# Linear attention and two MoE layers on one core: program order for the regular part of layer 1, with side work, stores and a weight reload moved

## The chip, the core and the metric

The kernel runs on one core of a Trainium2 chip. The metric is the device time of one execution in microseconds, lower is better. The core has five engines with a queue of instructions each: TensorE (PE; its weight loads are listed apart, as PEld), VectorE (DVE), ScalarE (ACT), GpSimd (POOL) and SyncE (SP). SyncE and GpSimd issue the DMA transfers here. Engines wait for each other by semaphores; an engine that waits holds up everything behind it in its own queue.

## The reference

Three stages follow each other on 4608 tokens (8 batches of 576) of 512 features (8 heads of 64).

```python
kv  = einsum('bhsd,bhse->bhde', k, v)          # 64 x 64 for each batch and head
out = einsum('bhsd,bhde->bhse', q, kv)
x   = out / sqrt(mean(out * out, -1) + 1e-6) * g_norm
h = x @ w_in;   x = (h * sigmoid(1.702 * h)) @ w_out       # layer 1, 512 to 2048 to 512
h = x @ w2_in;  y = (h - tanh(h)) @ w2_out                 # layer 2, the same sizes
```

## The kernel before, in words

**Tiles.** A tile is one batch, 576 tokens. For each of the two layers (`l`) and eight tiles (`n`) the kernel runs two matrix products on TensorE: `m1` (line 520, called M1 here) multiplies by w_in and `m2` (line 635, M2) by w_out. Each takes seven products of sums of quarters in place of eight quarter products, and each of those is made in three fp16 passes (high by high, high by low, low by high). M1 and M2 each have 336 matmuls of 128x128 by 128x288; these are called regular matmuls here. They add up in the PSUM banks `X`, `Y` and `Z`, two of each. Tile (0,0) is computed by plain products (`m1_plain`, `m2_plain`). Tiles are written (layer, number); the regular part of layer 1 is (0,2) to (0,7).

**M2.** It has 28 steps of 12 matmuls (line 680 on), four for each of the products 2, 1, 5, 6, 7, 3, 4 in this order (`ORDER2`); products 2 and 3 add up in Y, 5 in Z, the others in X. The weights come from DRAM as 14 blocks of 512 KB into four buffers `st` (`stream`, line 629, issued on SyncE). Each block serves two steps, 24 matmuls; when its steps are written, the next block that uses its buffer is issued (`FREED2`):

```python
for _ in range(min(FREED2.get(i, 0), 14 - len(pre))):
    pre.append(stream(l, len(pre)))
```

The operand `jt` comes from the activations `gt` by ScalarE (line 605) and VectorE (line 611). In layer 1 results go to `x2d` in DRAM by `store` (line 641, SyncE), and `x2load` (line 340, SyncE) brings them back for layer 2.

**Attention as side work.** While M2 of tile n of layer 1 runs, `front` (line 364) does the first half of the attention for tile n + 2, in four units of two heads: k-by-v products (line 385, 10 passes on TensorE), copies of the result to `kv` (lines 388 and 389, ScalarE), numerators q by kv (line 397), their squares rounded and exact (lines 409 and 410, ScalarE), the difference of the two (line 413, VectorE), sums of the squares over features as matmuls with `sel` (line 421), mean squares (line 424), and after the last unit the roots. While M1 of tile n + 1 runs, `back` (line 473) does the second half: `newton` (lines 441 to 450, the last of its steps gives `hl`, line 449), spreads of the inverse roots over the features (line 456, TensorE, bank `AT`), products with the numerators (line 460), and `xprep` (line 306), which writes the fp16 operand `xo` of the next M1. K-by-v products, numerators, sums and spreads share the two banks `AT`.

**Layer 2's weights.** `conv1` (line 191) converts them during layer 1, 32 items with loads and stores on GpSimd's queue and their arithmetic mostly on VectorE. When M2 of (0,7) has been written, the eight tiles `wi` of w_in are reloaded with layer 2's (line 949, SyncE).

**Order.** Side work is made of generators. `add_side(g, a, b)` registers one, and `tick` lets it advance `a` times in each step of M1 and `b` times in each step of M2; a `yield` in a generator thus sets a distance in steps. `issue_after` keeps a piece of side work behind marked main instructions. `drain` runs a generator to its end. What is written in this order is then placed by a scheduler, engine by engine, except where `tc.manual_schedule(engines=...)` is entered: there the named engines keep the order of the program. Before the change that holds for TensorE and SyncE in layer 2 alone:

```python
if l == 1:
    ...
    man.enter_context(tc.manual_schedule(engines=frozenset([mybir.EngineType.PE, mybir.EngineType.SP])))
```

Of the kernel before, what the change touches and what calls it, by code (L numbers as in the profile page):

```python
# [8 lines left out]
F32 = mybir.dt.float32  # L9
# [73 lines left out]
def body(ctx, tc, att, gn, con, w_in, w_out, w2_in, w2_out, outT):  # L83
# [279 lines left out]

    def front(b, places=None, banks=None):

        if not places and b not in ahead:
            yield from fetch(b)  # L370
        for u, (kt, i) in enumerate(UNITS):
# [4 lines left out]
            K = A[u % 2]  # L376
            if places:
                unit = places[u]
                q, kv = unit[:, 0:T], unit[:, T:UNIT]
            else:  # L380
                qb, kb = ahead[b]
                q, kv = qb.ap, kb.ap
            kv = kv.rearrange("p (w c d) -> p w c d", w=2, c=5)
# [5 lines left out]
            nc.scalar.copy(out=d[64:128, 64:128], in_=K[64:128, 64:128])  # L389
            if not places:  # L390
                kb.free()
                if u < 3:
                    kb = yield from part(b, u + 1, T, UNIT)
            yield
            yield
            for j in range(2):
                nc.tensor.matmul(out=A[j][:, 0:H], lhsT=d, rhs=q[:, j * H:(j + 1) * H], start=True, stop=True)
            if places:
                sq = unit[:, T:2 * T]
            else:  # L400
                qb.free()
                if u < 3:
                    qb = yield from part(b, u + 1, 0, T)
                    ahead[b] = qb, kb
                ex = yield from scr.need(T)
                sq = ex.ap
            for j in range(2):
# [5 lines left out]
            nc.vector.tensor_tensor(out=slr, in0=sq, in1=shr.bitcast(F32), op=ALU.subtract)  # L413
            if not places:
                ex.free()
            yield
# [8 lines left out]
            yield  # L425
            if b == 0 and u % 2:
                yield u // 2
        if b:
            y = yield from scr.need(H)
            t = yield from scr.need(H)  # L430
            yt[:] = y, t
            roots(slice(0, P))
            nc.scalar.activation(out=dummy, in_=t.ap[:, 0:1], func=AF.Gelu_apprx_sigmoid)
        yield
# [38 lines left out]
    def back(b, dst):  # L473

        hi, hl = shr[:, 0:H], slr[:, 0:H]
        yield from newton(slice(0, P), hi, hl)
        for x in yt:
            x.free()
        for u, (kt, i) in enumerate(UNITS):
            yield from scaled_unit(b, u, hl, slice(0, P), AT)  # L480
            if i == 1:
                ex = yield from scr.need(3 * H)
                yield from xprep(xbs[b, kt], ex, dst[:, kt])
                if kt == 0 and b < NS - 1:
                    yield from fetch(b + 1)


# [147 lines left out]
    def m2(l, n, tails, pre):  # L635
# [5 lines left out]
        def store(qd, ob, ds):  # L641

            m, j = qd // 2, qd % 2
            src = ob.ap[:, :T].rearrange("p (d f) -> p d f", d=2)[:, ds]
            dst = (x2d if l == 0 else outT.rearrange("(k p) f -> k p f", p=P))
            dst = dst[2 * m:2 * m + 2, :, n * T + j * H:n * T + (j + 1) * H].rearrange("d p f -> p d f")[:, ds]
            main((nc.sync if l == 0 or n == NS - 1 else nc.gpsimd).dma_start(out=dst, in_=src))

# [10 lines left out]
        def quad(qd, d, name):  # L659
# [4 lines left out]
            if d == 1:  # L664
                cc.pop(name).free()

        def fin(r, d):
# [16 lines left out]
            elif r == 4:  # L684
                scaled(x, d, 4)
                quad(2, d, 4)

        for i in range(28):
            r, pp = STEPS2[i]
            s = pre[ORDER2.index(r) * 2 + pp // 2]  # L690
# [16 lines left out]
            for _ in range(min(FREED2.get(i, 0), 14 - len(pre))):  # L707
                pre.append(stream(l, len(pre)))
            if i == 0:
                tail1()  # L710
            elif i == 1:
                tail2()
            elif i == 2:
                flush()
                flush()
                jcap[0] = 28
            jadvance(i + 1 + LA)
            tick(1)


# [130 lines left out]
    def both0():  # L851

        yt[:] = scr(H), scr(H)
        chains = [front(0, room, banks)]
        while chains:
# [20 lines left out]
    for l in range(2):  # L876
        for n in range(NS):
            bk = fr = None
            if l == 0:
# [4 lines left out]
                elif n < NS - 1:  # L884
                    bk = add_side(back(n + 1, xo[(n + 1) % 2]), 0.6, 1.0)
                else:
# [3 lines left out]
            if (l, n) == (0, 2):  # L890
                add_side(later, 0.85, 0.0)

# [15 lines left out]
            if l == 1:  # L908
                fixed[0] = True
                marks.clear()  # L910
                marks.update({k: m for k, m in latest.items() if k == mybir.EngineType.DVE})
                man.enter_context(tc.manual_schedule(engines=frozenset([mybir.EngineType.PE, mybir.EngineType.SP])))
            if (l, n) == (0, 0):
# [28 lines left out]
            if l == 0 and 1 <= n < NS - 2:  # L942
                drain([bk])
                fr = add_side(front(n + 2), 0.0, 1.1)
            m2(l, n, tails, pre)
            if l == 0 and n == NS - 1:
                drain([later])
                for p in range(NP):
                    nc.sync.dma_start(out=wi[p], in_=wid[p])
            drain([bk, fr])  # L950
# [42 lines left out]
```

## Time and profile before

| | us |
|---|---|
| time, median of 3 runs | 1516.06 |
| lowest and highest of the runs | 1514.57, 1516.18 |
| the profiled execution | 1515.95 |
| its span | 1514.2 |
| TensorE busy | 1459.4 (96%) |
| VectorE busy | 1184.3 (78%) |
| ScalarE busy | 945.7 (62%) |
| GpSimd busy | 134.7 (9%) |
| mean DMA rate | 155 GB/s |

How to read it: the span is the part of the profiled execution from its first to its last instruction, and all places in the trace are microseconds from its start. Busy shares are averages over stages; a stage is read from a window that is cut at its first and last matmul. The records of TensorE overlap, since a matmul of 0.29 us starts every 0.12 us; the distance of starts is what one costs. The column PEclk is the clock that TensorE was granted, as a share of 2.4 GHz: 1.00 is that level and 0.50 is 1.2 GHz. A wait is put down to the instruction that came last.

### The profile page before, as it was taken

Reading aid. Unit: us, or ns where it says so; the run is one execution under the profiler, and the core shown is the slowest. Engines: PE = TensorE matmul, PEld = TensorE weight load, DVE = VectorE, ACT = ScalarE, POOL = GpSimd, SP = SyncE. Lnnn points to the kernel's source line nnn. Section 1 sums busy time; section 2 is a strip of 40 time slices with the busy share of each in tenths; the row PEclk is TensorE's granted clock in tenths of the full one; section 3 lists DMA queues with packets and bytes.
Section 4 is the critical chain, followed back from the end, with each engine's and each line's share of the span. In section 5 each row is a group of like instructions: output and inputs, shape, how many; then the busy total and the mean of one; then the engine's idle time right before and its main releaser. Section 6 shows DMA issues by size and latency. Waiting matters only on the chain.

```text
span 1514.2 us, 29446 instructions
## 1 busy us (share of the span) xinstructions
PE 1459.4 (96%) x11508; PEld 1159.8 (77%) x11508; DVE 1184.3 (78%) x2357; ACT 945.7 (62%) x2075; POOL 134.7 (9%) x209
## 2 busy tenths in 40 slices
PE   6979799999999999999999999999999999999999
PEld 5667577777787877877677777777777777777777
DVE  4999979497796987959858686877777787868585
ACT  5766586676777767767556465646565565656463
POOL 0000010022223221211100000000000000000000
PEclk8899899999999999999999999999999999999999
DMA  8684415447567475672576415070614333241504
GB/s 310 208 249 128 147 62 196 140 132 250 165 209 234 128 253 178 199 237 70 185 250 231 148 59 192 15 231 22 195 56 156 111 118 125 86 142 44 184 15 157
DMA packets 96525, 235.36 MB, mean 155 GB/s; under 512 B 10112, under 2 KB 49152, under 8 KB 96384
## 3 DMA queue, kind: packets, MB, share of 16 engines
q1 hardware_dynamic: 78848, 165.95, 34.1%
q0 software_dynamic: 17536, 67.51, 13.4%
q8 instruction: 90, 1.47, 0.4%
q14 instruction: 51, 0.42, 0.1%
HBM read 191.48 MB, written 41.94 MB: 154 GB/s over the span
## 4 chain that ended last, share of the span: by engine, by line
PE 78%; DMA 8%; DVE 8%; ACT 3%; issue 3%; POOL 0%; SPq 0%; ACTq 0%; DVEq 0%; POOLq 0%
PE X L530 7%; PE X L702 7%; PE X L704 7%; PE X L703 7%; PE X L532 7%; PE X L531 7%; PE Y L702 4%; PE Y L704 4%; PE Y L703 4%; PE Z L530 3%; PE Z L532 3%; PE Z L531 3%; DMA st<-wod 3%; PE Z L702 2%; PE Z L704 2%
## 5 line engine op out<-in xcount | busy, mean ns | idle before, releaser
L611 DVE SCALAR_TENSOR_TENSOR jt<-gt,jt 128x576 f16<-128x576 f32 x420 | 312.6, 753 | 106.9 <-ACT jt L605 103.1
L605 ACT ACTIVATE jt<-gt 128x576 f16<-128x576 f32 x420 | 284.6, 684 | 156.0 <-PE X L704 56.6
L530 PE MATMUL X<-xo,wi 128*128 128x288 f16 x960 | 274.6, 286 | 7.4 <-ACT mscratch L563 4.7
L531 PE MATMUL X<-xo,wi 128*128 128x288 f16 x960 | 274.7, 286 | 2.1 <-DVE xo L323 2.1
L532 PE MATMUL X<-xo,wi 128*128 128x288 f16 x960 | 274.6, 286 | 0.0
L703 PE MATMUL X<-jt,st 128*128 128x288 f16 x960 | 274.2, 286 | 0.0
L704 PE MATMUL X<-jt,st 128*128 128x288 f16 x960 | 274.0, 286 | 0.0
L702 PE MATMUL X<-jt,st 128*128 128x288 f16 x960 | 273.4, 286 | 0.0
L702 PEld LDWEIGHTS <-st 128*128 128x128 f16 x1680 | 165.0, 98 | 60.8 <-DMA st<-wod 17.2
L563 ACT COPY mscratch<-X 128x288 f32<-128x288 f32 x360 | 141.2, 396 | 106.1 <-PE X L532 92.6
L531 PEld LDWEIGHTS <-wi 128*128 128x128 f16 x1680 | 164.7, 98 | 50.4 <-issue 8.2
L530 PEld LDWEIGHTS <-wi 128*128 128x128 f16 x1680 | 164.5, 98 | 47.1 <-issue 4.4
L703 PEld LDWEIGHTS <-st 128*128 128x128 f16 x1680 | 165.1, 98 | 43.4
L704 PEld LDWEIGHTS <-st 128*128 128x128 f16 x1680 | 165.2, 98 | 43.4 <-issue 0.3
L532 PEld LDWEIGHTS <-wi 128*128 128x128 f16 x1680 | 164.5, 98 | 44.3 <-issue 2.5
L591 DVE TENSOR_TENSOR gt<-gt 128x576 f32<-128x576 f32 x240 | 176.7, 749 | 1.4 <-ACT gt L537 1.1
L702 PE MATMUL Y<-jt,st 128*128 128x288 f16 x480 | 136.2, 289 | 10.3 <-DMA st<-wod 10.3
L568 DVE TENSOR_TENSOR mscratch<-Z,mscratch 128x288 f32<-128x288 f32 x240 | 108.1, 452 | 38.5 <-ACT mscratch L563 22.2
L703 PE MATMUL Y<-jt,st 128*128 128x288 f16 x480 | 137.9, 288 | 0.0
L704 PE MATMUL Y<-jt,st 128*128 128x288 f16 x480 | 137.5, 288 | 0.0
L530 PE MATMUL Z<-xo,wi 128*128 128x288 f16 x480 | 137.5, 286 | 0.0
L531 PE MATMUL Z<-xo,wi 128*128 128x288 f16 x480 | 137.4, 286 | 0.0
(238 smaller groups left out, 2572.0 us busy)
## 6 DMA issues: line engine op xcount, KB each, us to landing
st<-wod SPq DMA_DIRECT2D x210, 512.0 KB, 4.7
scratch<-att POOLq DMA_DIRECT2D x28, 640.0 KB, 4.8
scratch<-x2d SPq DMA_DIRECT2D x32, 288.0 KB, 5.9
cbk<-w_out POOLq DMA_DIRECT2D x32, 256.0 KB, 4.3
cbk<-w_in POOLq DMA_DIRECT2D x32, 256.0 KB, 4.1
scratch<-att POOLq DMA_DIRECT2D x28, 288.0 KB, 4.5
x2d<-mscratch SPq DMA_DIRECT2D x28, 288.0 KB, 5.4
outT<-mscratch POOLq DMA_DIRECT2D x28, 288.0 KB, 5.0
```

The source lines that it names most:

```text
L530: nc.tensor.matmul(out=out, lhsT=wh, rhs=xh, start=fresh and kt == 0, stop=False, skip_group_check=k)
L531: nc.tensor.matmul(out=out, lhsT=wh, rhs=xl, start=False, stop=False, skip_group_check=k)
L532: nc.tensor.matmul(out=out, lhsT=wl, rhs=xh, start=False, stop=kt == 1, skip_group_check=k)
L563: main(nc.scalar.copy(out=b.ap, in_=x))
L568: main(nc.vector.tensor_tensor(out=b.ap, in0=add[0], in1=b.ap, op=ALU.add))
L591: tt = lambda o, a, b: main(nc.vector.tensor_tensor(out=G[:, :, o, :], in0=G[:, :, a, :], in1=G[:, :, b, :], op=ALU.subtract))
L605: main(nc.scalar.activation(out=j[:, :, 0, :], in_=GT[STEPS2[i][1]][:, :, QD[STEPS2[i][0]], :], func=AF.Copy, scale=SX))
L611: main(nc.vector.scalar_tensor_tensor(out=j[:, :, 1, :], in0=GT[STEPS2[i][1]][:, :, QD[STEPS2[i][0]], :], scalar=SX, in1=j[:, :, 0, :], op ...
L702: nc.tensor.matmul(out=out, lhsT=wh, rhs=xh, start=a, stop=False, skip_group_check=k)
L703: nc.tensor.matmul(out=out, lhsT=wh, rhs=xl, start=False, stop=False, skip_group_check=k)
L704: nc.tensor.matmul(out=out, lhsT=wl, rhs=xh, start=False, stop=z, skip_group_check=k)
```

## The change

- TensorE and SyncE keep the program's order in tiles (0,2) to (0,7) too.
- `front` is rewritten (batch 0 keeps the old form as `front0`): the k-by-v products of the next unit stand right beside the sums of squares of this one, and two yields stand between each of the other parts.
- `back` gets two yields behind `newton` and one more after each unit; its rate in M1 goes from 0.6 to 0.72, and that of `front` in M2 from 1.1 to 1.05.
- `conv1` advances 0.62 in a step of M1 and 0.5 in a step of M2, where it was 0.85 and 0.
- Stores of x2d are kept in a list and issued three steps later (`due`); their scratch is freed then.
- The reload of `wi` becomes side work of M2 of (0,7), on GpSimd's queue, at 0.4 in a step.

The diff, cut to its core (the rest of `front0` loses the branches that batch 0 does not take):

```diff
--- before.py
+++ after.py
...
-    def front(b, places=None, banks=None):
-
-
-
-
-        if not places and b not in ahead:
-            yield from fetch(b)
+    def front0(b, places, banks):
...
+    def kv_product(b, u, kv, K):
+
+        kv = kv.rearrange("p (w c d) -> p w c d", w=2, c=5)
+        for c in range(5):
+            nc.tensor.matmul(out=K[:, 0:P], lhsT=kv[:, 0, c, :], rhs=kv[:, 1, c, :], start=(c == 0), stop=(c == 4))
+        d = kvt[UNITS[u][1]]
+        nc.scalar.copy(out=d[0:64, 0:64], in_=K[0:64, 0:64])
+        nc.scalar.copy(out=d[64:128, 64:128], in_=K[64:128, 64:128])
+
+    def numerators(u, q, A):
+        for j in range(2):
+            nc.tensor.matmul(out=A[j][:, 0:H], lhsT=kvt[UNITS[u][1]], rhs=q[:, j * H:(j + 1) * H], start=True, stop=True)
+
+    def mean_squares(u, K, pairs):
+        n = 2 * len(pairs[0])
+        ks = [(sel[:, 98 - 32 * u - 2 * j:226 - 32 * u - 2 * j], s) for j in range(2) for s in pairs[j]]
+        for k, (w, s) in enumerate(ks):
+            nc.tensor.matmul(out=K[:, 0:H], lhsT=w, rhs=s, start=k == 0, stop=k == n - 1)
+        rows = slice(32 * u, 32 * u + 32)
+        nc.scalar.activation(out=ms[rows, :], in_=K[rows, 0:H], func=AF.Identity, bias=eps[rows, :])
+
+    def front(b):
+
+        if b not in ahead:
+            yield from fetch(b)
+            yield
+            yield
+        qb, kb = ahead[b]
+        kv_product(b, 0, kb.ap, AT[0])
+        kb.free()
+        kb = yield from part(b, 1, T, UNIT)
+        yield
+        for u, (kt, i) in enumerate(UNITS):
+            if i == 0:
+                xbs[b, kt] = yield from scr.need(4 * H)
+            og = xbs[b, kt].ap[:, i * T:(i + 1) * T]
+            ex = yield from scr.need(T)
+            sq = ex.ap
+            numerators(u, qb.ap, AT)
+            qb.free()
+            for j in range(2):
+                c = slice(j * H, (j + 1) * H)
+                nc.scalar.activation(out=sq[:, c], in_=AT[j][:, 0:H], func=AF.Square)
+                nc.scalar.activation(out=shr[:, c], in_=AT[j][:, 0:H], func=AF.Square)
+                nc.scalar.activation(out=og[:, c], in_=AT[j][:, 0:H], func=AF.Copy, scale=gsc)
+            if u < 3:
+                qb = yield from part(b, u + 1, 0, T)
+            yield
+            yield
+            nc.vector.tensor_tensor(out=slr, in0=sq, in1=shr.bitcast(F32), op=ALU.subtract)
+            ex.free()
+            yield
+            yield
+            mean_squares(u, AT[u % 2], [[s[:, j * H:(j + 1) * H] for s in (shr, slr)] for j in range(2)])
+            if u < 3:
+                kv_product(b, u + 1, kb.ap, AT[(u + 1) % 2])
+                kb.free()
+                if u < 2:
+                    kb = yield from part(b, u + 2, T, UNIT)
+            yield
+            yield
+        y = yield from scr.need(H)
+        t = yield from scr.need(H)
+        yt[:] = y, t
+        roots(slice(0, P))
+        nc.scalar.activation(out=dummy, in_=t.ap[:, 0:1], func=AF.Gelu_apprx_sigmoid)
...
@@ -476,13 +517,22 @@
         yield from newton(slice(0, P), hi, hl)
         for x in yt:
             x.free()
+        yield
+        yield
         for u, (kt, i) in enumerate(UNITS):
             yield from scaled_unit(b, u, hl, slice(0, P), AT)
+            yield
             if i == 1:
                 ex = yield from scr.need(3 * H)
                 yield from xprep(xbs[b, kt], ex, dst[:, kt])
                 if kt == 0 and b < NS - 1:
                     yield from fetch(b + 1)
+
+    def reload():
+
+        for p in range(NP):
+            nc.gpsimd.dma_start(out=wi[p], in_=wid[p])
+            yield
 
@@ -644,7 +694,10 @@
             src = ob.ap[:, :T].rearrange("p (d f) -> p d f", d=2)[:, ds]
             dst = (x2d if l == 0 else outT.rearrange("(k p) f -> k p f", p=P))
             dst = dst[2 * m:2 * m + 2, :, n * T + j * H:n * T + (j + 1) * H].rearrange("d p f -> p d f")[:, ds]
-            main((nc.sync if l == 0 or n == NS - 1 else nc.gpsimd).dma_start(out=dst, in_=src))
+            if l == 0:
+                late.append((step_[0] + 3, dst, src, ob))
+            else:
+                main((nc.sync if n == NS - 1 else nc.gpsimd).dma_start(out=dst, in_=src))
 
         def fma(out, ps, b):
             main(nc.vector.scalar_tensor_tensor(out=out, in0=ps, scalar=inv, in1=b, op0=ALU.mult, op1=ALU.add))
@@ -662,7 +715,9 @@
             elif d == 1:
                 store(qd, cc[name], slice(0, 2))
             if d == 1:
-                cc.pop(name).free()
+                ob = cc.pop(name)
+                if l == 1:
+                    ob.free()
 
         def fin(r, d):
             x, y, z = X[d][:, 0:H], Y[d][:, 0:H], Z[d][:, 0:H]
@@ -685,7 +740,16 @@
                 scaled(x, d, 4)
                 quad(2, d, 4)
 
+        step_, late = [0], []
+
+        def due(i):
+            while late and late[0][0] <= i:
+                _, dst, src, ob = late.pop(0)
+                main(nc.sync.dma_start(out=dst, in_=src))
+                ob.free()
+
         for i in range(28):
+            step_[0] = i
             r, pp = STEPS2[i]
             s = pre[ORDER2.index(r) * 2 + pp // 2]
             jadvance(i + 1)
@@ -706,6 +770,7 @@
                     fin(r, d)
             for _ in range(min(FREED2.get(i, 0), 14 - len(pre))):
                 pre.append(stream(l, len(pre)))
+            due(i)
             if i == 0:
                 tail1()
             elif i == 1:
@@ -716,6 +781,7 @@
                 jcap[0] = 28
             jadvance(i + 1 + LA)
             tick(1)
+        due(99)
 
 
     QW = {(0, 0): 1, (0, 1): 2, (1, 0): 3, (1, 1): 0}
@@ -882,13 +948,13 @@
                 elif n == 1:
                     bk = add_side(both(2, xo[0]), 1.5, 0.8)
                 elif n < NS - 1:
-                    bk = add_side(back(n + 1, xo[(n + 1) % 2]), 0.6, 1.0)
+                    bk = add_side(back(n + 1, xo[(n + 1) % 2]), 0.72, 1.0)
                 else:
                     bk = add_side(x2load(0, xo[0]), 0.4, 0.8)
             elif n < NS - 1:
                 bk = add_side(x2load(n + 1, xo[(n + 1) % 2]), 0.4, 0.8)
             if (l, n) == (0, 2):
-                add_side(later, 0.85, 0.0)
+                add_side(later, 0.62, 0.5)
 
             def hook(p):
                 if (l, n) == (0, 0):
@@ -909,6 +975,8 @@
                 fixed[0] = True
                 marks.clear()
                 marks.update({k: m for k, m in latest.items() if k == mybir.EngineType.DVE})
+                man.enter_context(tc.manual_schedule(engines=frozenset([mybir.EngineType.PE, mybir.EngineType.SP])))
+            elif n >= 2:
                 man.enter_context(tc.manual_schedule(engines=frozenset([mybir.EngineType.PE, mybir.EngineType.SP])))
             if (l, n) == (0, 0):
                 m1_plain(hook)
@@ -941,12 +1009,11 @@
             pre = [stream(l, i) for i in range(4)]
             if l == 0 and 1 <= n < NS - 2:
                 drain([bk])
-                fr = add_side(front(n + 2), 0.0, 1.1)
-            m2(l, n, tails, pre)
+                fr = add_side(front(n + 2), 0.0, 1.05)
             if l == 0 and n == NS - 1:
                 drain([later])
-                for p in range(NP):
-                    nc.sync.dma_start(out=wi[p], in_=wid[p])
+                fr = add_side(reload(), 0.0, 0.4)
+            m2(l, n, tails, pre)
             drain([bk, fr])
             man.close()
 
```

Three places show how the instructions move. First TensorE in M2 of tile (0,4), around product 3. `X_82` and `X_83` are the two banks of X (halves of the output features), `Y_84` and `Y_85` those of Y; line 421 is the sum of squares before, line 420 the numerators after. Before, product 3 in Y follows product 6 in X:

```order
L704 LDWEIGHTS st
L704 MATMUL X_83<-jt,st 128x288
L421 MATMUL AT_88<-sq_103,sel 128x288
L702 LDWEIGHTS st
L702 MATMUL Y_84<-jt,st 128x288
```

After, it stands behind product 7's last matmuls, and numerators stand between them:

```order
L768 LDWEIGHTS st
L768 MATMUL X_83<-jt,st 128x288
L420 MATMUL AT_88<-scratch,kv_107 128x288
L420 MATMUL AT_89<-scratch,kv_107 128x288
L766 LDWEIGHTS st
L766 MATMUL Y_84<-jt,st 128x288
```

The first step of product 3, 12 matmuls, moved from before product 7 to behind its 48 matmuls. The sums of squares and the next unit's k-by-v products (line 413 after) now stand together on TensorE in the same M2:

```order
L426 MATMUL AT_88<-sq_103,sel 128x288
L426 MATMUL AT_88<-sq_104,sel 128x288
L413 MATMUL AT_89<-scratch 128x128 x5
L766 LDWEIGHTS st
L766 MATMUL X_82<-jt,st 128x288
```

Before, they stood apart, with regular matmuls between. Second, VectorE at the start of M1 in a tile of the regular part. Lines 568 (before) and 618 (after) are M1's additions, 444, 445 and 449 (before) and 485, 486 and 490 (after) are `newton`, the last of them `hl`; the rows on `cbk` are the conversion. Before:

```order
L444 TENSOR_TENSOR scratch<-scratch,ms 128x288
L445 SCALAR_TENSOR_TENSOR scratch<-scratch 128x288
L568 TENSOR_TENSOR mscratch<-Y_84,mscratch 128x288
L568 TENSOR_TENSOR mscratch<-Y_85,mscratch 128x288
L611 SCALAR_TENSOR_TENSOR jt<-gt_73,jt 128x2x288
L568 TENSOR_TENSOR mscratch<-Z_86,mscratch 128x288
L173 TENSOR_TENSOR cbk<-cbk 128x7x128
L449 SCALAR_TENSOR_TENSOR sq_104<-sq_103,low,scratch 128x288
```

After:

```order
L167 TENSOR_TENSOR cbk<-cbk 128x128
L168 TENSOR_TENSOR cbk<-cbk 128x128
L169 TENSOR_TENSOR cbk<-cbk 128x128
L170 TENSOR_TENSOR cbk<-cbk 128x128
L618 TENSOR_TENSOR mscratch<-Y_84,mscratch 128x288
L490 SCALAR_TENSOR_TENSOR sq_104<-sq_103,low,scratch 128x288
```

The step that makes `hl` moved from behind the third addition to behind the first. Third, SyncE in M2 of (0,7). Before, the reload of `wi` (line 949) stands among the loads of x2d (line 344); `wi_63` to `wi_70` are its eight tiles:

```order
L949 DMA wi_63<-wid 128x3584
L949 DMA wi_64<-wid 128x3584
L344 DMA scratch<-x2d 128x576 x2
L949 DMA wi_65<-wid 128x3584
L949 DMA wi_66<-wid 128x3584
L949 DMA wi_67<-wid 128x3584
L949 DMA wi_68<-wid 128x3584
L344 DMA scratch<-x2d 128x576
```

After (line 682 is the stream, 748 the store):

```order
L748 DMA x2d<-mscratch 128x2x288
L682 DMA st<-wod_92 128x2048 x5
L748 DMA x2d<-mscratch 128x2x288 x3
L344 DMA scratch<-x2d 128x576 x4
L682 DMA st<-wod_92 128x2048 x4
L344 DMA scratch<-x2d 128x576 x4
L682 DMA st<-wod_92 128x2048 x5
```

The reloads are gone from this queue, and the loads of x2d stand between streams.

## Rows read from the trace of the kernel before

**Rows 1.** The page's head and its busy time of TensorE.
```profile
span 1514.2 us, 29446 instructions
...
PE 1459.4 (96%) x11508; PEld 1159.8 (77%) x11508; DVE 1184.3 (78%) x2357; ACT 945.7 (62%) x2075; POOL 134.7 (9%) x209
```

**Rows 2.** Windows by tile, (0,2) on; columns by engine, then clock, DMA, GB/s.
```profile
core 0: us, PE busy (x) PEld busy (x) DVE busy (x) ACT busy (x) POOL busy (x), PEclk, DMA share, GB/s
...
384.80:479.80 95.00, 94.20 (x754) 75.74 (x753) 79.49 (x158) 71.05 (x157) 23.86 (x34) 1.00 0.63 201
...
676.80:766.00 89.20, 85.65 (x683) 67.20 (x680) 72.15 (x143) 53.42 (x112) 9.00 (x14) 0.98 0.47 152
...
933.30:1015.70 82.40, 82.40 (x675) 65.77 (x673) 64.42 (x125) 46.84 (x101) 2.85 (x4) 1.00 0.36 115
285.20:850.50 565.30, 550.95 (x4362) 438.80 (x4360) 451.29 (x891) 387.04 (x846) 93.23 (x139) 0.99 0.59 190
```

**Rows 3.** TensorE's waits, tiles (0,2) to (0,7): us, times, longest.
```profile
PE Y L702 <- DMA st<-wod: 9.1, 5, 2.5
PE Z L702 <- DMA st<-wod: 4.4, 2, 2.3
```

**Rows 4.** Chain of waits in M2 of (0,4): start, us, what.
```profile
549.10 0.14 PE X L704
...
549.25 6.42 DMA st<-wod
...
555.72 0.30 PE Y L702
```

**Rows 5.** Windows at stalls and behind them, columns as above.
```profile
351.10:354.50 3.40, 3.40 (x16) 1.92 (x14) 3.18 (x6) 3.12 (x8) 1.99 (x3) 0.50 1.01 372
552.90:555.60 2.70, 0.36 (x3) 0.14 (x1) 2.70 (x8) 1.53 (x4) 0.00 (x0) 1.00 0.88 327
555.90:559.30 3.40, 3.40 (x17) 2.53 (x16) 0.26 (x2) 0.63 (x2) 1.39 (x2) 0.50 0.69 216
...
830.50:832.80 2.30, 0.34 (x3) 0.03 (x1) 1.97 (x4) 1.04 (x3) 0.00 (x0) 1.00 0.59 221
832.80:836.20 3.40, 3.33 (x28) 2.67 (x29) 0.76 (x1) 0.68 (x1) 0.00 (x0) 1.00 0.31 100
```

**Rows 6.** Stream transfers' landing, M2 of (0,2), then of (0,4).
```profile
DMA to landing us min/median/max: 3.7/5.2/8.8
...
DMA to landing us min/median/max: 4.0/5.3/6.6
```

**Rows 7.** TensorE's waits from layer 2 on.
```profile
PE X L530 <- ACT mscratch L563: 0.4, 1, 0.4
```

**Rows 8.** Timelines of TensorE and ScalarE, M2 of (0,4).
```profile
518.80 0.29 PE L702 MATMUL Y<-jt,st 128*128 128x288 f16 x1
...
526.10 0.21 ACT L389 COPY kv<-AT 64x64 f32<-64x64 f32 x1
```

**Rows 9.** Timelines of TensorE and VectorE, unit 3 in (0,2).
```profile
373.40 1.13 PE L397 MATMUL AT<-scratch,kv 128*128 128x288 f32 x4
...
378.97 0.76 DVE L413 TENSOR_TENSOR sq<-scratch,sq 128x576 fp32r<-128x576 f32 x1 [3.16 <-ACT sq L410]
```

**Rows 10.** Timelines of TensorE and VectorE, M1 of (0,3).
```profile
384.83 0.29 PE L530 MATMUL Z<-xo,wi 128*128 128x288 f16 x1
...
394.92 0.51 DVE L449 SCALAR_TENSOR_TENSOR sq<-sq,low,scratch 128x288 fp32r<-128x288 f32 x1
```

**Rows 11.** SyncE's queue waits, tiles (0,2) to (0,7).
```profile
SPq L949 <- PE Z L532: 24.2, 8, 8.4
...
SPq L647 <- DVE mscratch L650: 16.1, 13, 3.1
```

**Rows 12.** Windows, M2 of (0,1), and TensorE's waits before 285.2.
```profile
226.80:285.20 58.40, 57.16 (x453) 46.16 (x450) 40.67 (x73) 36.22 (x84) 4.85 (x9) 1.00 0.63 203
...
PE Y L421 <- DVE sq L413: 2.6, 1, 2.6
```

More of the change, by code (lines that the diff above doesn't have):

```diff
@@ L376, in front @@
             K = A[u % 2]
[L377 to L382, printed above, removed]
+            unit = places[u]
+            q, kv = unit[:, 0:T], unit[:, T:UNIT]
             kv = kv.rearrange("p (w c d) -> p w c d", w=2, c=5)
@@ L389, in front @@
             nc.scalar.copy(out=d[64:128, 64:128], in_=K[64:128, 64:128])
[L390 to L393, printed above, removed]
             yield
@@ L397, in front @@
                 nc.tensor.matmul(out=A[j][:, 0:H], lhsT=d, rhs=q[:, j * H:(j + 1) * H], start=True, stop=True)
[L398 to L406, printed above, removed]
+            sq = unit[:, T:2 * T]
             for j in range(2):
@@ L413, in front @@
             nc.vector.tensor_tensor(out=slr, in0=sq, in1=shr.bitcast(F32), op=ALU.subtract)
-            if not places:
-                ex.free()
             yield
@@ L425, in front @@
             yield
-            if b == 0 and u % 2:
+            if u % 2:
                 yield u // 2
[L428 to L433, printed above, removed]
+    def kv_product(b, u, kv, K):
[5 more added lines that the diff above has]
+        nc.scalar.copy(out=d[64:128, 64:128], in_=K[64:128, 64:128])
@@ L853, in both0 @@
         yt[:] = scr(H), scr(H)
-        chains = [front(0, room, banks)]
+        chains = [front0(0, room, banks)]
         while chains:
```

## The prediction

> **What bounds the kernel now.** I read the page's head first: TensorE is busy in 1459.4 us of a 1514.2 us span [rows 1], so a change pays only where TensorE stands or runs at its lower clock. The profiled execution took 1515.95 us, 1.75 more than its span and 0.11 below the median of 1516.06; the sum below starts from 1515.95. A measurement of this kernel can tell about 0.2%, 3 us, from no change.
>
> Then the windows by tile, cut at the first matmul of each tile [rows 2]. A tile of layer 2 has 672 regular matmuls and takes 82.4 us where nothing disturbs it: 0.1226 us for each. In tile (0,3) TensorE is busy 94.2 of 95.0, so attention's work there costs 94.2 - 82.4 = 11.8. Of the six tiles (0,2) to (0,7) four have both halves of the attention, (0,6) has the spreads and products only, 683 records on TensorE to layer 2's 675, so 8 more at about 0.12 us, an estimate of 1.0, and (0,7) has none: 4 x 94.2 + 83.4 + 82.4 = 542.6 us without loss. They take 565.3 [rows 2]: 22.7 us are lost there, and this is all that the order of the regular part can give.
>
> Where they go is in TensorE's waits over that stretch: 9.1 us before Y and 4.4 before Z of M2, seven times, each for a streamed block of w_out [rows 3], 13.5 together; all else in that view is small. The chain of waits shows how one comes about, in M2 of (0,4): an X matmul ends at 549.25, a transfer of 6.42 us follows, and the Y matmul starts at 555.72 [rows 4]. The buffer came free only as TensorE reached the work that needed it: product 3 (Y) had been put ahead of product 7 (X), which follows it in the code and whose blocks were there. Four of these stalls are followed by a stretch of 3.4 us at granted clock 0.50, the 1.2 GHz level, with 16 or 17 matmuls in it (two of the four stand in the rows). The stall of 2.0 us at 830.5 was not: the same length behind it holds 28 at 1.00 [rows 5]. Half speed for 3.4 us loses 1.7, four times 6.8; by the missing matmuls, 11 x 0.1226 = 1.35 each, it would be 5.4. I take 6.8. 13.5 + 6.8 = 20.3 of the 22.7.
>
> **The change part by part.** *Program order on TensorE and SyncE, -13.5 and -6.8.* Product 3 goes back behind product 7, so a stream buffer is released 72 regular matmuls before it is read, 72 x 0.1226 = 8.8 us with side work on top. Blocks landed in 5.2 us in the median and 8.8 at worst in M2 of (0,2), 5.3 and 6.6 in that of (0,4) [rows 6]; the worst just fits. Layer 2 already runs in this order: from 850.5 on TensorE waits 0.4 us in all [rows 7]. It has less side work, so this speaks for the streams and not for the attention. With the stalls go the low-clock stretches behind them. I take both in full; the least is half of them, if blocks come late (below).
>
> *Numerators of unit 0, +2.0.* In the new order they stand 36 regular matmuls into M2, 36 x 0.1226 = 4.4 us plus about 1.1 of products, so 5.5 after its start. They need the copies of k-by-v out of PSUM, behind ScalarE's own work. Now M2 of (0,4) starts at 518.80 and its second copy ends at 526.31, 7.5 after [rows 8]. As late as that, each of four tiles waits 2.0; but the products come earlier now, before M2's first matmul, so the copies may be in time. I take 0.5 each; bounds 0 and 8.
>
> *Sums of squares, 0.* They stand 48 regular matmuls (5.9 us) behind the numerators. The longest lag I found in the regular part is unit 3 of (0,2): numerators at 373.40, subtraction done at 379.73, 6.3 from start to end and 5.2 from the end of the numerators [rows 9]. That fits by 0.7. The two copies of k-by-v, 0.2 each [rows 8], have 24 matmuls (2.9 us). Bound: 0.5 in each of 16 units, 8.
>
> *Spreads of the back half, 0.* The first stands at 54 matmuls of M1, 6.6 us. It needs `hl`, Newton's last result. In (0,3) M1 begins at 384.83 and `hl` is done at 395.43, 10.6 after [rows 10]: at that lateness TensorE would stand 4.0 us, and with it everything behind. I take 0 because the new DVE order puts `hl` right behind the first of M1's additions instead of the third, about 18 matmuls in, which leaves 36 matmuls (4.4 us) for what else DVE has queued. This is the weakest term; its bound is the rival below.
>
> *Late stores, 0.* A store of x2d that waits for its last addition holds up the blocks queued behind it on SyncE: 16.1 us in 13 waits, 3.1 at most [rows 11]. Issued three steps (36 matmuls) later it finds its data ready; the gain is inside the stream term, since those blocks were not what TensorE waited for. Its scratch comes free 4.4 us later; nothing on TensorE waits for that.
>
> *Weight reload on GpSimd's queue, 0.* Eight transfers of 896 KB, on SyncE now, where they wait 24.2 us behind the last use of each weight [rows 11], ahead of streams. They leave that queue. The bytes in M2 of (0,7) stay the same, and eight issues by step 20 leave eight steps, 11.8 us, until layer 2 needs the first. The Trainium skill says in "DMA: Bandwidth & Descriptors", section "Issuing engines are not separate DMA queues", that transfers of all issuers interleave on the same 16 engines; by that the reload still takes its share from the streams there. No row separates them.
>
> *Conversion of layer 2's weights over M1 and M2, 0.* The DVE items only move: DVE is busy 79.5 of 95.0 us in (0,3) [rows 2], 15 us of cover. If M2 has none left, DVE delays the subtractions; that is the bound of 8 above.
>
> *Early tiles, +1.* Tile (0,1) keeps the scheduler but gets the new front half. In its M2 TensorE is busy 57.2 of 58.4 us, so 1.2 is the most it can gain; the longest wait of the early part for this subtraction was 2.6 [rows 12]. Between -1.2 and +5.2 (twice that) I take 1.
>
> Sum: 1515.95 - 13.5 - 6.8 + 2.0 + 1.0 = 1498.65, **1499 us**, 1.1% faster. With no cost at the numerators and the early gain it is 1494; with one of the upper bounds (8 for 2.0) 1505.
>
> **The rivals.** *Blocks still come late (0.15).* Waits move but half of the 20.3 stays, 1499 + 10 = **1509**. For it: in the low-clock stretch at 351.10 the DMA share is 1.01 [rows 5], so the DMA engines were full, and the conversion's loads now run in M2 too. Against it: what (0,4) lacked was 72 matmuls of lead, not bandwidth.
>
> *TensorE stands at the spreads: slower (0.09).* If `hl` stays at 10.6 us, five tiles wait 4.0, 20.0, and stalls that long have been followed by the low clock, 5 x 1.7 = 8.5; 1498.65 + 28.5 = **1527**. It decides where `hl` comes later than about 6.6 + 2.3 = 8.9 us: from there each tile costs at least 2.3 + 1.7 = 4.0, five tiles 20, against a gain of 17.3. For it: where I looked it is that late now [rows 10], and the five tiles are built alike. Against it: its new place on DVE. The Trainium skill, "TensorE: Matmul & The Clock Gate", section "The mechanism", has matmuls strictly in order, none passing another. The trace agrees: at 552.90 TensorE is busy 0.36 of 2.70 us [rows 5] while product 7 stood ready behind the wait. By that rule a written order that is wrong in one place stops all of TensorE, which would give this rival's 1527.
>
> *Little or nothing changes (0.06), 1513.* Both attention bounds come true at once, 0.5 in each of 16 sums (8) and 8 for 2 at the numerators: 1498.65 + 14. Or program order is what the scheduler made anyway, and the time stays 1516; the order of the new kernel's instructions speaks against that.
>
> *More than forecast (0.04), 1492:* the sum without its two costs (3.0), with the last 2.4 of the 22.7, and the early part's 1.2.
>
> **How the numbers follow.** Forecast 0.66, own range 1494 to 1505. The range 1491 to 1511 takes in the late blocks and leaves out the slower rival and most of "nothing much". Faster by over 0.2%: 0.66 + 0.15 + 0.04 = 0.85, of which I leave 0.01 to early tiles that go worse than their bound; same 0.06; slower 0.09 + 0.01.
>
> **What would show it.** The waits of TensorE on streamed blocks should fall from 13.5 us to under 2, no stretch at 0.50 should be left in tiles (0,2) to (0,7), and those tiles should sum to about 547. Numerators waiting for kv copies over 0.5 us a tile, or spreads waiting for `hl` at all, show the two weak terms wrong. Spreads that wait over 2.3 us with a low-clock stretch behind them would make the prediction wrong; blocks that land later than 8.8 us would halve it.

## The result and the profile after

The changed kernel takes 1524.55 us in the median of 4 runs (1521.29 to 1525.35), the kernel before 1515.53 on the same chip: a ratio of 1.0056, 95% interval 1.0039 to 1.0073. It is slower by 0.6%, where 1499 and 1.1% faster was forecast; the time lies outside the range of 1491 to 1511. The profiled execution took 1525.35, 9.4 more than that of before.

The page's head and busy times first: the engines are as busy as before [rows 1] to within 2 us, but for 4.4 more on GpSimd, which has eight more instructions, the reload. Nothing else was added; TensorE stands longer.

```profile
span 1523.6 us, 29448 instructions
...
PE 1459.8 (96%) x11508; PEld 1160.0 (76%) x11508; DVE 1186.1 (78%) x2357; ACT 945.4 (62%) x2075; POOL 139.1 (9%) x217
```

In program order the first matmuls of M1 run before the last of the M2 ahead of it, so the windows are cut at the last M2 matmul of each tile here; the columns are those of [rows 2].

```profile
297.00:396.20 99.20, 95.74 (x762) 76.85 (x760) 80.88 (x164) 74.12 (x161) 21.62 (x31) 1.00 0.57 177
396.20:500.00 103.80, 97.61 (x757) 77.37 (x755) 81.73 (x163) 70.39 (x156) 25.66 (x37) 0.97 0.58 187
500.00:596.20 96.20, 94.69 (x755) 76.01 (x753) 81.11 (x163) 70.01 (x156) 20.65 (x31) 1.00 0.63 198
596.20:693.20 97.00, 94.77 (x755) 76.07 (x753) 80.80 (x162) 70.09 (x156) 18.21 (x29) 1.00 0.62 200
693.20:778.30 85.10, 83.35 (x676) 66.05 (x675) 69.16 (x137) 51.92 (x111) 7.05 (x11) 1.00 0.44 143
778.30:860.70 82.40, 82.40 (x674) 65.77 (x673) 57.52 (x104) 49.96 (x107) 4.27 (x8) 1.00 0.71 240
297.00:860.70 563.70, 548.56 (x4366) 438.13 (x4364) 451.20 (x891) 386.49 (x845) 97.46 (x147) 0.99 0.59 191
```

Two things are read from them. (0,2) begins at 297.0 where it began at 285.2 before: the early tiles lost 11.8 us. And the regular part of layer 1 takes 563.7 for 565.3, a gain of 1.6 where 18.3 was forecast. Layer 2 is 0.8 shorter. Tile (0,7) runs at 82.4, as an undisturbed one; (0,3) went from 95.0 to 103.8.

One execution is one sample. Four of the runs below have this kernel's order, on every engine, up to (0,2) or beyond; in their traces (0,2) begins at 292.1, 295.1, 295.2 and 295.3, while with the order of before it begins between 282.8 and 285.2. So the early loss is there in all of them, but its size differs by some 5 us between executions. In the regular part single tiles of one order differ by up to 2.5 us (the run on (0,6) and (0,7), below), so the gain of 1.6 there is no more than scatter.

TensorE's waits from M2 of (0,1) to the end of layer 1 say what took the place of the 13.5 us on streamed blocks [rows 3]. The first two rows are copies out of bank X by ScalarE (line 613 in M1, 709 in M2); the last two lie in M2 of (0,1).

```profile
PE X L580 <- ACT mscratch L613: 8.4, 10, 1.4
PE X L766 <- ACT mscratch L709: 6.5, 4, 4.8
PE Z L766 <- DMA st<-wod: 4.2, 1, 4.2
PE AT L420 <- DMA scratch<-att: 3.6, 1, 3.6
```

The longest, 4.8 us in (0,3), is followed back in three timelines, of TensorE, ScalarE and GpSimd (in brackets: idle before, and what ended it).

```profile
471.11 0.29 PE L768 MATMUL X<-jt,st 128*128 128x288 f16 x1
476.19 0.40 PE L766 MATMUL X<-jt,st 128*128 128x288 f16 x1 [4.79 <-ACT mscratch L709]
```
```profile
470.43 0.54 ACT L453 ACTIVATE scratch<-AT,gsc 128x288 f32<-128x288 f32 x1
474.61 0.66 ACT L152 ACTIVATE cbk<-cbk 128x512 f32<-128x512 f32 x1 [3.65 <-DMA cbk<-w_out]
475.17 0.67 ACT L655 ACTIVATE jt<-gt 128x576 f16<-128x576 f32 x1
475.74 0.69 ACT L709 ACTIVATE mscratch<-X 128x288 f32<-128x288 f32 x2
```
```profile
458.85 1.57 POOL L216 DMA_DIRECT2D wod<-cbk  x2 [1.01 <-DVE cbk L173]
467.87 0.71 POOL L140 DMA_DIRECT2D cbk<-w_out  x1 [7.45 <-DMA wod<-cbk]
```

GpSimd stores a converted piece at 458.85 and waits 7.45 us until it has landed, since the next load goes to the same place; that load is issued at 467.87. ScalarE has the conversion's first step (line 152) next in its queue and stands 3.65 us for the load, with the copy out of X behind it. TensorE's next product (7) adds up in X right behind product 6, and in program order nothing may go ahead of it. All three stalls of over 3 us had the 1.2 GHz level behind them, the last already from within:

```profile
256.00:259.40 3.40, 3.31 (x14) 2.11 (x15) 1.39 (x3) 0.21 (x1) 0.00 (x0) 0.50 0.04 15
269.70:273.10 3.40, 3.05 (x10) 2.19 (x11) 0.00 (x0) 1.58 (x4) 0.00 (x0) 0.50 0.07 27
474.50:481.30 6.80, 5.12 (x22) 3.27 (x22) 4.95 (x10) 3.08 (x6) 1.43 (x2) 0.50 0.56 188
```

### The profile page after: what moved, and what is told of

The parts are those of the page before. It is cut to its first block, busy times and chain, and to the rows that moved or that the text cites. A ratio compares the mean times of both kernels' runs of the same rounds, so it can differ in the third digit from the quotient of the medians.

```text
span 1523.6 us, 29448 instructions
## 1 busy us (share of the span) xinstructions
PE 1459.8 (96%) x11508; PEld 1160.0 (76%) x11508; DVE 1186.1 (78%) x2357; ACT 945.4 (62%) x2075; POOL 139.1 (9%) x217
## 4 chain that ended last, share of the span: by engine, by line
PE 48%; issue 21%; DVE 7%; ACT 4%; DMA 2%; POOL 1%; POOLq 0%; ACTq 0%; DVEq 0%
PE X L766 5%; PE X L767 5%; PE X L768 5%; PE X L580 4%; PE X L582 4%; PE X L581 4%; PE Y L766 2%; PE Y L768 2%; PE Y L767 2%; PE Z L580 2%; PE Z L582 2%; PE Z L581 2%; DVE jt L661 1%; DVE gt L641 1%; PE Y L580 1%
## 5 line engine op out<-in xcount | busy, mean ns | idle before, releaser
L580 PE MATMUL Z<-xo,wi 128*128 128x288 f16 x480 | 137.7, 287 | 0.1
L581 PE MATMUL Z<-xo,wi 128*128 128x288 f16 x480 | 137.5, 287 | 0.0
L582 PE MATMUL Z<-xo,wi 128*128 128x288 f16 x480 | 137.4, 286 | 0.0
L768 PE MATMUL Y<-jt,st 128*128 128x288 f16 x480 | 137.2, 286 | 0.0
L767 PE MATMUL Y<-jt,st 128*128 128x288 f16 x480 | 137.2, 286 | 0.0
```

What stands on the lines that cost most here:

```text
L580: nc.tensor.matmul(out=out, lhsT=wh, rhs=xh, start=fresh and kt == 0, stop=False, skip_group_check=k)
L581: nc.tensor.matmul(out=out, lhsT=wh, rhs=xl, start=False, stop=False, skip_group_check=k)
L582: nc.tensor.matmul(out=out, lhsT=wl, rhs=xh, start=False, stop=kt == 1, skip_group_check=k)
L767: nc.tensor.matmul(out=out, lhsT=wh, rhs=xl, start=False, stop=False, skip_group_check=k)
L768: nc.tensor.matmul(out=out, lhsT=wl, rhs=xh, start=False, stop=z, skip_group_check=k)
```

## The experiments

Theory A: the stream stalls are gone as forecast, but the copies out of X on ScalarE take their place, the largest by the conversion's late load, and the new front half costs about 10 us in (0,1), where the scheduler still places it. Rivals: program order itself costs it; the late stores hold scratch that copies need.

**Program order alone.** On the kernel before:

```diff
+            elif n >= 2:
+                man.enter_context(tc.manual_schedule(engines=frozenset([mybir.EngineType.PE, mybir.EngineType.SP])))
```

> The kernel before with program order for TensorE and SyncE in tiles (0,2) to (0,7) and nothing else. If the order does what the prediction took it to do and the loss comes from the other parts, the 13.5 us of waits on streamed blocks and the 6.8 of low clock go, less some new waits of side work whose distances were not written for this order: 1497 to 1507. If program order itself costs what it brings, 1512 to 1525, with waits on kv copies, subtractions or hl in TensorE's list.

Measured 1545.93, ratio 1.0218 [1.0194, 1.0242], outside both. TensorE's waits from 282.8 to 900:

```profile
PE Z L530 <- DMA wi<-wid: 10.3, 1, 10.3
PE AT L397 <- ACT kv L389: 6.7, 2, 4.0
PE X L530 <- ACT mscratch L563: 5.2, 8, 2.3
PE AT L456 <- DVE sq L449: 5.0, 5, 1.7
PE AT L421 <- DVE sq L413: 4.6, 4, 1.9
```

The streams are down to one wait of 1.8. In their place stand numerators, spreads (for `hl`, five times) and sums of squares, each too near to what it needs, and at the start of layer 2 a wait of 10.3 for the reload, which program order on SyncE puts behind all of the last tile's streams. In the changed kernel only the waits for copies out of X are left of these. So its other parts aren't extras: together they remove waits that program order brings. Which part removes which was run apart only for the back half in (0,6), below.

**Conversion in M1 alone**, on the changed kernel: `add_side(later, 0.85, 0.0)` for `0.62, 0.5`.

> The changed kernel with the conversion's rates set back to 0.85 and 0. Theory: in M2 of (0,3) a conversion instruction on ScalarE waits for its late load, and the copy out of bank X stands behind it; that costs 4.8 us and a low clock of 6.8 us, 3.4. Then this wait falls under 1 us, the low-clock stretch in (0,3) goes, and the time is 1524.5 - 8.2 = 1516 (1514 to 1519). Rival: the copy waits for scratch that the late stores still hold; then the wait and 1524 stay.

Measured 1520.76, ratio 1.0050 [1.0031, 1.0069]. The 4.8 us wait and its low clock are gone, yet the regular part still takes 562.1 (292.1 to 854.2) for 563.7. This trace is 4.6 shorter than the changed kernel's, mostly by its early tiles, which have the same order in both. TensorE's waits for copies out of X come to 6.0 and 4.0 for 8.4 and 6.5, and it is busy 548.8 us with no stretch at 0.50, where two runs below without such a stretch need 546.0; where these 2.7 go was not found. ScalarE's waits at the conversion show that the change of rates is no cure; in the changed kernel, then in this one, then in the kernel before:

```profile
ACT cbk L152 <- DMA cbk<-w_out: 3.6, 1, 3.6
```
```profile
ACT cbk L152 <- DMA cbk<-w_out: 6.9, 4, 3.0
...
ACT cbk L152 <- DVE cbk L173: 3.0, 6, 0.8
```
```profile
ACT cbk L152 <- DMA cbk<-w_out: 5.2, 2, 3.1
ACT cbk L152 <- DVE cbk L173: 5.0, 10, 1.2
```

The rates don't remove ScalarE's waiting, they share it out. The kernel before had over 10 us of it, and TensorE lost 0.4 to copies of line 563 in that stretch.

**The early tiles as before:** the old front half for batches 1 to 3, no added yields for batches 1 and 2.

```diff
+        if b > 2:
             yield
             yield
...
-                fr = add_side(front(n + 2), 0.0, 1.05)
+                fr = add_side((front_old if n == 1 else front)(n + 2), 0.0, 1.1 if n == 1 else 1.05)
```

> The changed kernel with the old front half for batches 1 to 3 and no extra yields in the back half for batches 1 and 2, so that every engine's order up to tile (0,2) is the one of before. Theory: the new front half, placed by the scheduler in tiles (0,0) and (0,1), costs 12 us; then (0,2) starts at 285 in place of 297 and the time is about 1512.5 (1510 to 1516). Rival: the late stores or what follows cost it; then (0,2) still starts at 292 or later and the time stays above 1518.

Measured 1515.14, ratio 1.0002 [0.9982, 1.0022]: M2 of (0,1) ends at 284.7, 12.3 us earlier than in the changed kernel's trace, as theory A has it. The regular part is 565.3; the ScalarE stall now stands in (0,4), 5.1 us with a low clock of 6.8.

**Stores at once,** on the changed kernel: `store` issues and frees as before.

> The changed kernel with the stores of x2d issued at once, as before. Theory (the stores neither cost nor give): 1522 to 1527, the wait of X for the ScalarE copy in (0,3) still over 4 us. Rival (the late stores pin scratch that the copies need): that wait under 1 us and 1514 to 1517.

Measured 1525.14, ratio 1.0077 [1.0059, 1.0096]. The time is the changed kernel's. ScalarE's copies in M1 wait less for scratch that stores still hold, 1.2 us for 4.7 in the regular part, but TensorE's waits for them stay, 8.6 for 8.4: the rival is out. What the late stores give is small: without them a product in X of (0,6) waits 1.8 for its block, and the tile takes 87.1 for 85.1. The longest wait for line 709 was 2.4 here, between the two forecasts, at the same place in (0,3). TensorE, VectorE, ScalarE and GpSimd have the changed kernel's order in this run, so one order can give a stall of 4.8 with a low clock behind it or one of 2.4 with none: ScalarE stood 1.3 for the load, not 3.65. The regular part is 561.9.

**Both: early tiles as before, conversion in M1.**

> Both of the last: the early tiles as before, and the conversion's rates 0.85 and 0. Theory (the early tiles cost about 10 us, the conversion's late load in M2 5 us and a low clock of 3.4): 1515 less 8 = 1507 (1504 to 1510), and no low clock in tiles (0,2) to (0,7). Rival (the conversion costs ScalarE time wherever it stands, and the stall moves into M1): 1511 to 1515.

Measured 1518.47, ratio 1.0021 [0.9999, 1.0043]: a miss. No low clock is left in the regular part, but it takes 565.7; waits for copies out of X come to 7.6 and 5.3, where the early tiles as before alone had 9.8 and 7.6, and ScalarE stands 6.9, 2.1 and 3.0 at line 152. The rival has the stall move into M1; the waits there fell. What is won is given back: TensorE waits 2.9 for VectorE and 1.0 for a load of k and v, and is busy 548.4 for 547.7 although the low clock is gone; why was not found.

**The conversion's first step without the wait for its load.** The load stays, but the step reads a constant tile; layer 2's converted weights are left out.

```diff
-            yield from words(1, R[k % 2], wb)
+            yield from words(1, sel[:, 0:1024].bitcast(F32), wb)
```

> The changed kernel, in which the conversion's first step reads a constant tile instead of the words that were loaded (what layer 2 multiplies by is then not its weights; loads, stores, arithmetic and the order on all engines stay). Theory: ScalarE stands at that step for the load, 3.65 us in (0,3), and TensorE behind it; without the wait the 4.8 us stall and the low clock of 6.8 us in (0,3) go: 1524.5 - 8.2 = 1516 (1513 to 1518). Rival (ScalarE is late by its own work, not by the load): 1522 to 1526.

Measured 1518.07, ratio 1.0028 [1.0009, 1.0046]. The time is at the edge of the theory's range. The order of every engine is that of the changed kernel; one wait is out. The regular part falls from 563.7 to 557.6, waits of X in M2 from 6.5 to 2.6, and M1's stay:

```profile
PE X L580 <- ACT mscratch L613: 8.7, 11, 1.4
PE X L766 <- ACT mscratch L709: 2.6, 4, 1.0
```

So the late load costs 6.1 by these two traces, 4.3 against the run with the stores at once. What is left stands behind ScalarE's own work in line ahead of a copy, such as this in M1 of (0,5) of the changed kernel, where TensorE's next product in X waited 0.9 for the last row:

```profile
613.33 1.25 ACT L320 ACTIVATE xo<-scratch 128x576 f16<-128x576 f32 x2
614.47 0.92 ACT L208 CAST cbk<-cbk 128x896 f16<-128x896 f32 x1
615.30 0.40 ACT L613 COPY mscratch<-X 128x288 f32<-128x288 f32 x1
```

A copy out of X has two steps of M1, 12 matmuls or 1.5 us, until the same bank is wanted; xprep's pieces and the cast take 2.2 together.

**ScalarE in program order too.**

> The changed kernel with ScalarE in program order too in tiles (0,2) to (0,7). If TensorE waits for copies out of X because the scheduler puts side work ahead of them on ScalarE, these waits (9.3 and 6.5 us) fall to under 4 together and the time is 1510 to 1516. If ScalarE then stands at waits that the scheduler had kept out of its way, 1525 to 1545.

Measured 1570.8, ratio 1.0374 [1.0335, 1.0413], beyond both. The order of the program is worse on ScalarE than the scheduler's: waits for line 613 rise to 34.5, 26 of them.

**Program order from (0,1) on.**

> The changed kernel with program order from tile (0,1) on. Theory: the early loss is the scheduler's own placing of the new front half in M2 of (0,1), which puts a Z product and numerators ahead of their loads (4.2 and 3.6 us, each with a low clock behind); in program order these two waits go and (0,2) starts at 289 or earlier, time 1513 to 1518. Rival: the new front half brings late loads of q, k and v whatever the order; the wait for att of 3 us or more stays, and the time stays above 1520.

Measured 1530.07, ratio 1.0107 [1.0067, 1.0146], a miss. The two loads' waits are gone, as theory A said, but M1 of (0,1) now waits for its operand (5.8 for line 323), the spreads' bank (5.6 for line 501) and layer 1's converted weights `wi` (3.9 and 3.1), and M2 of (0,1) ends at 304.0. With this front half the scheduler's freedom is worth more there than it costs.

**The old front half for batch 3 alone.**

> The changed kernel with the old front half for batch 3 alone, the one in M2 of (0,1). If that one placement makes the early loss (waits of 4.2 and 3.6 us there, each with a low clock), (0,2) starts 8 to 9 us earlier than in the changed kernel, and the time is 1515 to 1517. If the loss comes with batches 1 and 2 and the back half's yields, it starts 3 or less earlier, and the time is 1521 to 1525.

Measured 1522.7, ratio 1.0053 [1.0031, 1.0075]. The start is the first expectation's, the time the second's. M2 of (0,1) ends at 288.3, 8.7 earlier than in the changed kernel's trace, but only 3.8 to 7.0 earlier than in the four runs of its early order; so this one placement is a good part of the early loss, and how large a part the traces can't tell. (0,2) then gives 5.9 of it back: 105.1 for 99.2, with a wait of 3.0 for `hl` and a low clock of 6.8 that begins within it. The regular part takes 565.6. What batches 1 and 2 cost wasn't taken apart.

**Program order in (0,6) and (0,7) alone,** on the kernel before, with the back half's yields and rate for (0,6) and the reload on GpSimd.

> The kernel before with program order, the extra yields of the back half and the reload on GpSimd in tiles (0,6) and (0,7) alone, where there is no front half. Theory: these two tiles take 85.1 and 82.4 us as in the changed kernel, against 89.2 and 84.5, and nothing else moves: 6.2 us faster than before, about 1508 to 1510. Rival: what comes before them shifts and gives it back, or ScalarE's conversion work holds up M1 of (0,6): no difference.

Measured 1512.06, ratio 0.9990 [0.9970, 1.0010]. Windows of these two tiles, then (0,7) before; (0,6) before is in [rows 2]:

```profile
673.70:762.70 89.00, 84.94 (x682) 66.60 (x680) 72.37 (x143) 54.41 (x112) 9.02 (x14) 1.00 0.44 142
762.70:845.10 82.40, 82.40 (x674) 65.75 (x673) 57.64 (x104) 49.84 (x107) 4.27 (x8) 1.00 0.74 242
```
```profile
766.00:850.50 84.50, 82.47 (x674) 65.67 (x672) 57.46 (x104) 49.13 (x107) 0.00 (x0) 1.00 0.67 223
```

(0,7) gains its 2.1; (0,6) only 0.2, where a product in X waits 2.0 for its block and 1.2 for copies out of X, and 0.7 go to VectorE. No spread waits for `hl` in (0,6), where program order alone had a wait of 1.4, so there it is the back half's yields and rate that take it away. The regular part is 561.6, 3.7 less, but 1.4 of that lies in tiles (0,2) to (0,5), where all engines have the order of before: a stall of 2.5 with a low clock in (0,5) is one of 1.7 without here. The times can't tell the gain from none.

**The conversion's first step on GpSimd,** on the kernel with the early tiles as before, then its cast too.

```diff
-        nc.scalar.activation(out=av, in_=rf[:, :, 1], func=AF.Copy, scale=2.0 ** -111)
+        if l:
+            nc.gpsimd.tensor_scalar(out=av, in0=rf[:, :, 1], scalar1=2.0 ** -111, scalar2=None, op0=ALU.mult)
+        else:
+            nc.scalar.activation(out=av, in_=rf[:, :, 1], func=AF.Copy, scale=2.0 ** -111)
...
-            nc.scalar.copy(out=d[:, :, 0, :], in_=B[:, 1:8])
+            nc.gpsimd.tensor_copy(out=d[:, :, 0, :], in_=B[:, 1:8])
```

> The kernel of e3 with the conversion's first step (the one that waits for its load) on GpSimd in place of ScalarE. Theory (ScalarE, standing at that load, holds up the copies out of X): the stall of 5.1 us in (0,4) and its low clock go, tiles (0,2) to (0,7) take about 557 in place of 565, and the time is 1515 - 8 = 1507 (1505 to 1510). Rival: GpSimd now waits there, and the loads of q, k and v behind it come late; then TensorE waits for att loads and the time is 1513 to 1520.

> As the last, with the conversion's cast (0.94 us on ScalarE, 32 of them) on GpSimd too. Theory: the cast and xprep stand ahead of the copies out of X in M1; without the cast those waits fall from about 10 us to 5, and the time is 1502 to 1506. Rival: GpSimd is slow at it or slows VectorE down; then waits for VectorE come, or (0,7) waits for the conversion's end, 1512 or more.

Measured 1507.9, ratio 0.9958 [0.9941, 0.9976], and 1506.16, ratio 0.9959 [0.9942, 0.9977]. Both beat the kernel before, and the changed one by about 1%. Waits for copies out of X in the first, then in the second, and the second's regular part:

```profile
PE X L657 <- ACT mscratch L690: 8.5, 10, 2.3
PE X L843 <- ACT mscratch L786: 0.9, 1, 0.9
```
```profile
PE X L657 <- ACT mscratch L690: 3.3, 4, 2.3
PE Z L657 <- DVE mscratch L695: 2.5, 6, 1.0
...
283.10:838.30 555.20, 547.45 (x4363) 437.50 (x4361) 467.44 (x891) 346.89 (x781) 197.33 (x210) 1.00 0.60 193
```

The stall in M2 goes with the first step, as theory A says (558.3 for 565.3), and M1's waits fall to 3.3 with the cast (555.2). VectorE is busy 467 for 451 us and makes TensorE wait 2.5, so the cast's gain is half given back: it shows in the trace, and the times don't tell the two apart.

The largest wait left, 2.3 us at the start of (0,2), shows how the scheduler had hidden ScalarE's lateness. The first copy out of X stands behind the roots, for which ScalarE loads its tables twice. TensorE and ScalarE of the last run, then ScalarE of the kernel before:

```profile
287.94 0.40 PE L657 MATMUL X<-xo,wi 128*128 128x288 f16 x1 [2.34 <-ACT mscratch L690]
```
```profile
283.87 1.28 ACT L554 ACT_TABLE_LOAD   x1
...
286.10 1.28 ACT L549 ACT_TABLE_LOAD   x1
...
287.51 0.38 ACT L690 COPY mscratch<-X 128x288 f32<-128x288 f32 x1
```
```profile
285.84 1.28 ACT L438 ACT_TABLE_LOAD   x1
...
289.47 0.38 ACT L563 COPY mscratch<-X 128x288 f32<-128x288 f32 x1
```

Up to this copy ScalarE has the same order in both, and the copy starts 4.3 us after M1's first matmul in both (283.23 and 285.20). Before, the scheduler had put other products ahead, and TensorE lost 0.2; in program order it loses 2.3, with a granted clock of 0.52 over the 3.4 us behind it (287.7 to 291.1).

## Why the prediction was wrong, by its own steps

- *What bounds the kernel:* right in the main; most of the 22.7 us lost in the regular part were waits on streams, and these are gone. *Program order, -13.5 and -6.8:* right for the streams, 13.5 to 0 in tiles (0,2) to (0,7), with blocks landing at 6.3 at worst in (0,4). (In the code product 7 stands ahead of product 3; one sentence of the prediction can be read the other way round, but its sum goes by the code.) Tiles (0,6) and (0,7) came out at 85.1 and 82.4 for 89.2 and 84.5. The low clock fell from four stretches of 3.4 to one of 6.8, at a stall of another cause.
- *The step that failed* is that no term stood for copies out of X: "all else in that view is small". That view showed what TensorE waited for while the scheduler could put another product ahead. ScalarE's lateness was there to read in its own waits, 10 us at line 152 of before, and in program order it reached TensorE: 8.4 + 6.5 in place of 0.4, and about 2.6 by the clock. Layer 2 was the evidence for program order, and "it has less side work" was drawn on for attention's matmuls, not for the queue of ScalarE. The rule that matmuls run strictly in order, from the Trainium skill, "TensorE: Matmul & The Clock Gate", section "The mechanism", was weighed at the spreads only; the trace agrees with it at 471.11 to 476.19, where TensorE starts no matmul.
- *Conversion, 0:* argued with VectorE's cover of 15 us, the wrong engine. Its late load holds ScalarE; without that wait the regular part is 6.1 shorter in one trace.
- *Early tiles, +1, bounds -1.2 to +5.2:* measured 11.8 (6.9 to 11.8 over the traces of this early order); 12.3 came back with the old code there. The waits were on loads (4.2 on a block, 3.6 on q) and the low clock, not on the subtraction that I bounded it by. A part that the scheduler places can be placed anew by any edit, and its bound should have been taken from the stalls of such placements elsewhere, 2 to 3 us each with 1.7 behind.
- *Numerators, +2, sums of squares, 0, and spreads, 0:* no wait for any of them in tiles (0,2) to (0,7), so 2.0 too much. In M1 of (0,4) `hl` is done at 502.83 and the first spread starts at 506.06:

```profile
502.32 0.51 DVE L490 SCALAR_TENSOR_TENSOR sq<-sq,low,scratch 128x288 fp32r<-128x288 f32 x1
```
```profile
506.06 0.52 PE L497 MATMUL AT<-sq,sel 128*128 128x288 f32 x2
```

- *The slower rival* was right in its sign and in its rule, wrong in its place: no spread waits in the changed kernel, so that its 1527 lies near the measured time is luck. With program order alone five spreads do wait for `hl` (5.0 us); that the rewritten back half takes this away is shown in (0,6) only.
- *Late stores, 0,* held within 2 us, by their own run. *Reload, 0,* held in the changed kernel; left on SyncE it would have cost 10.3 and a low clock.

The sum by the traces: 10.8 more than forecast in the early tiles, 16.7 in the regular part, 0.8 less in layer 2, together 26.7, the distance of 1525.35 from 1498.65. In the regular part -13.5, -6.8 + 2.6, and 14.5 of new waits for X make -3.2 for the measured -1.6. With the 5.4 that the missing matmuls gave for the low clock before, in place of 6.8, the sum is -1.8.

## What to carry to other kernels

Before an engine is put in program order, read the waits of the engines that feed it as well as its own: what the scheduler hides by reordering shows only there, and each such lateness is to be compared with the distance, in instructions, that the written order leaves it (here 12 matmuls, 1.5 us, in M1, and 6 matmuls, 0.7 us, from product 6 to product 7 of M2). A side step that waits for a transfer should stand on an engine whose queue holds nothing urgent. And an edit of code that the scheduler still places is an edit of that whole region, to be bounded by the stalls that such regions show.

## What the runs showed that I had not expected

The kernel before is not equally steady on every chip: its times were 1514.6 to 1516.2 beside the changed kernel and 1507.9 to 1522.5 beside the experiments. Windows of the trace show where a gain under 5 us lies, but each is one execution: with one order the early tiles end at 292.1 to 297.0. Putting 64 small pieces on GpSimd raised VectorE's busy time in the regular part by 16 us (451 to 467; 460 with the first 32) with the same count of instructions, 891; what causes that wasn't tried.
